# P.V with V as the moving operand in a two-layer decode attention kernel on one core

## Chip, core and metric

The kernel runs on one core of a Trainium2 chip. The metric is the device time of one execution in microseconds; the median of several runs counts.

## What is computed

Eight sequences (B = 8), one new token each, pass twice through an attention block and an MLP block with the same weights and the same K and V caches. D = 512, 32 query heads, 8 KV heads (four query heads share one), 8192 cached positions, head size 128; everything is bf16.

```python
def attention(x):                                  # x: [8, 1, 512]
    q = (x @ wq).reshape(8, 1, 32, 128).transpose(0, 2, 1, 3)
    k, v = repeat(k_cache, 4, axis=1), repeat(v_cache, 4, axis=1)
    p = softmax(einsum("bhqd,bhkd->bhqk", q, k) * 128 ** -0.5)
    return einsum("bhqk,bhkd->bhqd", p, v).transpose(0, 2, 1, 3).reshape(8, 1, 4096) @ wo
def mlp(x):                                        # w1: [512, 1792], w2: [1792, 512]
    return silu(x @ w1) @ w2
for _ in range(2):
    x = x + attention(layernorm(x))
    x = x + mlp(layernorm(x))
```

## The kernel before

The engines are called PE (TensorE), DVE (VectorE), ACT (ScalarE), POOL (GpSimd) and SP (SyncE, which issues the loads of K and V).

**Tasks and steps.** A task is one layer, one sequence and one KV head: 8192 positions, that is 64 chunks of 128. There are 2 x 8 x 8 = 128 tasks. A step handles 8 chunks, so a task has 8 steps (`GPT = 8`, `GRP = 8`). The loop at L616 runs over all steps in one fixed order, and every engine gets its instructions in that order.

**Loads.** K and V come in pieces of 512 KB (16 chunks, two steps) into 27 slots of one arena. A plan made beforehand fixes the order and the slot of each; SP issues a load as soon as the slot's last readers are done. In layer 0, K of the last 18 pieces of a sequence (of 32) stays in its slots, already transposed, and layer 1 uses it again. V is loaded in both layers. Per sequence `make_tasks` orders the tasks so: five tasks of layer 0 whose K is kept, three tasks of layer 1 of the sequence before, three tasks of layer 0 of the next sequence, and then five tasks of layer 1 with the kept K. Those last ones need no transposes, but for half of the first of them.

**A step `p`** gives out, in this order: the transposes of step `p + 3` (`emit_t`, L387: eight chunks of K against the identity into PSUM, from where DVE or ACT copies them back over K in the arena, L393 and L395); the scores of step `p` (`emit_s`, L418: each chunk of transposed K is the stationary operand and 32 query columns move, 4 of which count); P.V of step `p - 12` (`emit_pv`, L468: each chunk of V, 128 positions by 128, is the stationary operand, and four probability columns move); one part of the softmax of the task that has just got its scores; one stage of the chain, if one is open.

**Softmax.** In four steps after a task's last scores: maximum over the chunks on DVE (L427) and over partitions on POOL (L429); subtraction of the maximum on DVE from PSUM into the SBUF tile `SCs` (L436), then the exponential on ACT into `P` (L443); the sum on DVE and POOL; the reciprocal on DVE (L456). `P` has positions on its partitions and (chunk, head) on its columns.

**End of a task.** One step after a task's last P.V, `emit_norm` multiplies the output `OTp` in PSUM (128 head dimensions by 4 heads) by the reciprocal and writes it to `at1` or `at2` (L482).

**The chain.** When the last layer-0 task of a sequence is done, eleven stages are put up: output projection, layer norm, MLP, layer norm and the next query (`chain_of`, with `project` at L536 and `ln_stages`, whose last instruction is L524). One stage is given out a step, among the attention steps, and its matmuls move one column. The second layer of that sequence needs its result.

At the start X is loaded into `Xr` and turned by four small matmuls (L597); at the end the last blocks run for all eight sequences at once, L651 turns the result, and L658 copies it to `Xr` for the store.

Of the kernel before, what the change touches and what calls it, by code (L numbers as in the profile page):

```python
# [7 lines left out]
SM_SCALE = DH ** -0.5  # L8
# [4 lines left out]
GRP = 8  # L13
GPT = 8
# [5 lines left out]
LP = 12  # L20
# [7 lines left out]
BF16 = mybir.dt.bfloat16  # L28
FP32 = mybir.dt.float32
INT32 = mybir.dt.int32  # L30
ACT = mybir.ActivationFunctionType
# [157 lines left out]
def _build(ctx, nc, A_x, A_k_cache, A_v_cache, A_wq, A_wo, B_w1, B_w2, out):  # L189
    B, _sq, D = A_x.shape  # L190
# [3 lines left out]
    REP = HQ // HKV  # L194
    KT = D // 128
    FT = F // 128
    NCH = S // 128
# [10 lines left out]
    NG = len(tasks) * GPT  # L208

    pe = nc.tensor  # L210
    dve = nc.vector
    act = nc.scalar
    pool = nc.gpsimd
    sp = nc.sync
# [3 lines left out]
    def sb(shape, dt, name):  # L218
        _cnt[0] += 1
        return ctx.enter_context(nc.sbuf_tensor(f"{name}_{_cnt[0]}", shape, dt))  # L220

    def ps_bank(name, dt=FP32):
        _cnt[0] += 1
        n = 512 if dt == FP32 else 1024
        return ctx.enter_context(nc.psum_tensor(f"{name}_{_cnt[0]}", [128, n], dt))
# [3 lines left out]
    def chunk(slot, c):  # L229
        o = slot * SLOT + c * 128  # L230
        return ARENA[:, o:o + 128]

    def half(slot, h):
        o = slot * SLOT + h * GRP * 128
        return ARENA[:, o:o + GRP * 128]
# [3 lines left out]
    w1_sb = sb([128, KT, F], BF16, "w1")  # L239
    w2_sb = sb([128, FT, D], BF16, "w2")  # L240
    ident = sb([128, 128], BF16, "ident")
    Xr = sb([128, D], BF16, "X")
    XT = [sb([128, KT, B], BF16, f"XT{n}") for n in range(3)]
    QPAD = SW - REP
    QT1 = sb([128, B * HQ + QPAD], BF16, "QT1")
# [10 lines left out]
    xnT = sb([128, KT, B], BF16, "xnT")  # L256
    eh = sb([128, FT * B], FP32, "eh")
    hsT = sb([128, FT * B], BF16, "hsT")
    SCs = sb([128, NCH * REP], FP32, "SCs")
    Ps = [sb([128, NCH * REP], BF16, "P") for _ in range(NP)]  # L260
    mxp = [sb([128, REP], FP32, "mxp") for _ in range(NST)]
    mxa = [sb([128, REP], FP32, "mxa") for _ in range(NST)]
# [4 lines left out]
    SCp = [ps_bank("SCp") for _ in range(NSCP)]  # L267
    OTp = [ps_bank("OTp") for _ in range(2)]
    TPp = [ps_bank("TPp", BF16) for _ in range(NTP)]
    MISC = ps_bank("MISC")  # L270

    syn = Sync(nc, ctx)
    slsem = [DmaCounter(syn.new_sem(f"sl{i}")) for i in range(NSLOT)]
    wsem = {n: DmaCounter(syn.new_sem(f"w_{n}")) for n in ("wq", "wo", "w1", "w2", "x")}
    osem = syn.new_sem("osem")
# [3 lines left out]
    def res(name):  # L279
        if name not in R:  # L280
            R[name] = Res(name)
        return R[name]

    def r_half(slot, h):
        return res(f"slot{slot}_{h}")

    def op(eng, inst_fn, reads=(), writes=()):
        reads = [res(n) if isinstance(n, str) else n for n in reads]
        writes = [res(n) if isinstance(n, str) else n for n in writes]
        syn.acquire(eng, reads, writes)  # L290
        inst = inst_fn()
        tok = syn.mark(inst, eng)
        syn.release(tok, reads, writes)
        return tok

    def dma(eng, out_ap, in_ap, counter, reads=(), writes=()):
        reads = [res(n) if isinstance(n, str) else n for n in reads]
        writes = [res(n) if isinstance(n, str) else n for n in writes]
        syn.acquire(eng, reads, writes)
        tok = counter.next_tok()  # L300
        eng.dma_start(out_ap, in_ap).then_inc(counter.sem, 16)  # L301
        syn.release(tok, reads, writes)
        return tok

    def mm_group(steps, reads=(), writes=()):
        def run():
            inst = None
            for f in steps:
                inst = f()
            return inst  # L310
        return op(pe, run, reads, writes)

    x_in = A_x.rearrange("b s d -> (b s) d")
    out_v = out.rearrange("b s d -> (b s) d")
# [11 lines left out]
    with nc.Block() as block:  # L326

        @block.sync
        def _(sync_eng):
            dma(sp, Xr[0:B, :], x_in, wsem["x"], writes=["X"])  # L330

            op(pool, lambda: pool.memset(ident[:, :], 1.0), writes=["ident"])
            op(
# [4 lines left out]
                ),  # L338
                reads=["ident"], writes=["ident"],
            )  # L340
            op(pool, lambda: pool.memset(QT1[:, B * HQ:], 0.0), writes=["QT1"])
            for n in range(2):
                op(pool, lambda n=n: pool.memset(QT2[n][:, HQ:], 0.0), writes=[f"QT2_{n}"])
# [3 lines left out]
            def issue_until(pos):  # L347
                while queue and queue[0].after <= pos:
                    issue(queue.pop(0))
# [25 lines left out]
            def where(i):  # L375
                _l, b, g = tasks[i // GPT]
                return b, g, (i % GPT) // GPG, i % GPG
# [19 lines left out]
            def emit_t_until(i):  # L397
                while tnext[0] <= min(i, NG - 1):
                    if has_t(tnext[0]):
                        emit_t(tnext[0])  # L400
                    tnext[0] += 1
# [30 lines left out]
            def softmax_exp(ti):  # L432
                bank, st, pb = ti % NSCP, ti % NST, ti % NP
                op(
                    dve,
                    lambda: dve.tensor_tensor(  # L436
                        SCs[:, :].rearrange("p (c h) -> p c h", h=REP),
                        SCp[bank][:, 0:NCH * REP].rearrange("p (c h) -> p c h", h=REP),
                        mxa[st][:, :].unsqueeze(1).to_broadcast([128, NCH, REP]), ALU.subtract,
                    ),  # L440
                    reads=[f"SC{bank}", f"mxa{st}"], writes=["SCs"],
                )
                op(act, lambda: act.activation(Ps[pb][:, :], SCs[:, :], ACT.Exp, scale=SM_SCALE),  # L443
                   reads=["SCs"], writes=[f"P{pb}"])

            def softmax_sum(ti):
                st, pb = ti % NST, ti % NP
# [10 lines left out]
            def emit_pv(i):  # L458
                ti = i // GPT
                b, g, k, h = where(i)  # L460
                slot = v_slot[(b, g, k)]
                ob, pb = ti % 2, ti % NP
                otp = OTp[ob][:, 0:REP]
                steps = []
                for c in range(GRP):
                    cc = (i % GPT) * GRP + c
                    steps.append(
                        lambda c=c, cc=cc: pe.matmul(  # L468
                            otp, chunk(slot, h * GRP + c), Ps[pb][:, cc * REP:(cc + 1) * REP],
                            start=(cc == 0), stop=(cc == NCH - 1),  # L470
                        )
                    )
                mm_group(steps, reads=[r_half(slot, h), f"P{pb}"], writes=[f"OT{ob}"])

            def emit_norm(ti):
                layer, b, g = tasks[ti]
                ob, st = ti % 2, ti % NST
                if layer == 0:
                    dst, rd = at1[b % 2][:, g * REP:(g + 1) * REP], f"at1_{b % 2}"
                else:  # L480
                    dst, rd = at2[:, g * REP:(g + 1) * REP, b], "at2"
                op(dve, lambda: dve.tensor_tensor(dst, OTp[ob][:, 0:REP], rcp[st][:, :], ALU.mult),  # L482
                   reads=[f"OT{ob}", f"rcp{st}"], writes=[rd])
# [102 lines left out]
            def chain_of(b):  # L586
# [12 lines left out]
                        start=True, stop=True,  # L599
                    )  # L600
                    for kt in range(KT)
                ],
                reads=["X", "ident"], writes=["MISC"],
            )
            op(dve, lambda: dve.tensor_copy(XT[0][:, :, :], MISC[:, 0:KT * B].rearrange("p (k b) -> p k b", b=B)),
               reads=["MISC"], writes=["XT0"])
# [6 lines left out]
            last0 = {b: max(task_at[(0, b, g)] for g in range(HKV)) for b in range(B)}  # L613
            ntask = len(tasks)

            for p in range(NG + LP + GPT + 1):  # L616
                if p < NG:
                    layer, b, _g = tasks[p // GPT]
                    if layer == 1 and chain and chain_b[0] == b:
                        while chain:  # L620
                            chain.pop(0)()
                emit_t_until(p + LT)
                if p < NG:
                    emit_s(p)
                if 0 <= p - LP < NG:
                    emit_pv(p - LP)
                ti, ph = p // GPT - 1, p % GPT
                if 0 <= ti < ntask and ph < 4:
                    (softmax_max, softmax_exp, softmax_sum, softmax_rcp)[ph](ti)
                if chain:  # L630
                    chain.pop(0)()
                done = p - LP - GPT
                if done >= 0 and done % GPT == 0 and done // GPT < ntask:
                    tj = done // GPT
                    emit_norm(tj)
                    layer, b, _g = tasks[tj]
                    if layer == 0 and tj == last0[b]:
                        assert not chain
                        chain.extend(chain_of(b))
                        chain_b[0] = b  # L640
                issue_until(p)
            assert not queue and not chain

            for f in block_stages(
# [10 lines left out]
                ],  # L655
                reads=["XT0", "ident"], writes=["MISC"],
            )
            op(dve, lambda: dve.tensor_copy(Xr[0:B, :], MISC[0:B, :]), reads=["MISC"], writes=["X"])  # L658
            syn.acquire(sp, reads=[res("X")])
            sp.dma_start(out_v, Xr[0:B, :]).then_inc(osem, 16)  # L660
            sp.wait_ge(osem, 16)


# [26 lines left out]
```

## Time and profile before

| | |
|---|---|
| median of 3 runs (lowest to highest) | 1328.16 us (1327.6 to 1328.17) |
| span of the profiled execution | 1321.8 us |
| median less that span | 6.4 us |
| PE busy | 1009.8 us (76%), 25592 matmuls |
| DVE, ACT, POOL busy | 545.3, 328.8, 117.8 us |
| mean granted TensorE clock | 0.739 |
| HBM read | 473.44 MB |
| transposes L387 | 5888 matmuls, 128 moving columns |
| scores L418 | 8192 matmuls, 32 moving columns |
| P.V L468 | 8192 matmuls, 4 moving columns |
| chain and projections L536 | 3312 matmuls, 1 or 8 moving columns |

The profiled execution's own time is listed as its span; a time of the runs includes what lies around it. Matmuls are pipelined: the duration of one is longer than the distance to the next. The granted clock is a share of the full TensorE clock. "Issue" is time in which an engine waited for nothing that the profile shows.

### The profile page before, as it was taken

Reading aid. Unit: us, or ns where it says so; the run is one execution under the profiler, and the core shown is the slowest. Engines: PE = TensorE matmul, PEld = TensorE weight load, DVE = VectorE, ACT = ScalarE, POOL = GpSimd, SP = SyncE. Lnnn points to the kernel's source line nnn. Section 1 sums busy time; section 2 is a strip of 40 time slices with the busy share of each in tenths; the row PEclk is TensorE's granted clock in tenths of the full one; section 3 lists DMA queues with packets and bytes.
Section 4 is the critical chain, followed back from the end, with each engine's and each line's share of the span. In section 5 each row is a group of like instructions: output and inputs, shape, how many; then the busy total and the mean of one; then the engine's idle time right before and its main releaser. Section 6 shows DMA issues by size and latency. Waiting matters only on the chain.

```text
span 1321.8 us, 57028 instructions
## 1 busy us (share of the span) xinstructions
PE 1009.8 (76%) x25592; PEld 983.4 (74%) x25592; DVE 545.3 (41%) x1462; ACT 328.8 (25%) x414; POOL 117.8 (9%) x301
## 2 busy tenths in 40 slices
PE   3758867878677877778778886788867787788875
PEld 3757767877677877778778786787867787788874
DVE  2424434444343533444344442454434454344432
ACT  1323113312132222322123221331313222132210
POOL 0000010000000110000100001000010011000010
PEclk7878658858688776877678675886868867677765
DMA  8999899969999799997999889997999979999892
GB/s 342 386 399 403 291 371 408 377 230 398 408 407 376 256 407 407 408 344 286 408 408 395 303 344 407 408 383 275 377 408 407 388 243 407 407 406 357 287 408 112
DMA packets 133985, 477.14 MB, mean 361 GB/s; under 512 B 14176, under 2 KB 20080, under 8 KB 133232
## 3 DMA queue, kind: packets, MB, share of 16 engines
q1 hardware_dynamic: 133744, 473.51, 92.2%
q8 instruction: 203, 3.33, 1.0%
q14 instruction: 38, 0.31, 0.1%
HBM read 473.44 MB, written 0.01 MB: 358 GB/s over the span
## 4 chain that ended last, share of the span: by engine, by line
PE 53%; DMA 23%; issue 17%; DVE 5%; SPq 1%; POOL 1%; ACT 0%; POOLq 0%; DVEq 0%; ACTq 0%
PE TPp L387 24%; DMA arena<-in_A_k_cache_dram 18%; PE SCp L418 12%; PE OTp L468 11%; PE MISC L536 7%; DMA arena<-in_A_v_cache_dram 3%; SPq L301 1%; DVE arena L395 1%; DMA wq<-in_A_wq_dram 1%; DVE yr L522 1%; DVE tr L520 1%; DVE tr L519 1%; POOL s1a L507 0%; DVE xnT L524 0%; DVE yr L514 0%
## 5 line engine op out<-in xcount | busy, mean ns | idle before, releaser
L387 PE MATMUL TPp<-ident,arena 128*128 128x128 bf16 x5888 | 564.0, 253 | 109.2 <-DMA arena<-in_A_k_cache_dram 70.8
L387 PEld LDWEIGHTS TPp<-ident,arena 128*128 128x128 bf16 x5888 | 425.2, 113 | 117.4 <-DMA arena<-in_A_k_cache_dram 78.7
L395 DVE COPY arena<-TPp 128x1024 bf16<-128x1024 bf16 x460 | 317.3, 690 | 454.7 <-PE TPp L387 452.2
L393 ACT COPY arena<-TPp 128x1024 bf16<-128x1024 bf16 x276 | 278.6, 1010 | 688.6 <-PE TPp L387 688.6
L418 PE MATMUL SCp<-QT,arena 128*128 128x32 bf16 x8192 | 394.2, 184 | 68.6 <-issue 65.6
L468 PE MATMUL OTp<-P,arena 128*128 128x4 bf16 x8192 | 361.0, 165 | 79.3 <-issue 69.7
L418 PEld LDWEIGHTS SCp<-QT,arena 128*128 128x128 bf16 x8192 | 338.8, 103 | 71.0 <-issue 67.5
L468 PEld LDWEIGHTS OTp<-P,arena 128*128 128x128 bf16 x8192 | 290.7, 100 | 91.8 <-issue 81.0
L443 ACT ACTIVATE P<-SCs 128x256 bf16<-128x256 f32 x128 | 53.4, 417 | 271.4 <-DVE SCs L436 216.6
L429 POOL PARTITION_ALL_REDUCE mxa<-mxp x128 | 47.7, 373 | 727.0 <-DVE mxp L427 722.9
L451 POOL PARTITION_ALL_REDUCE ssa<-ssm x128 | 55.2, 431 | 296.4 <-DVE ssm L448 273.9
L427 DVE TENSOR_REDUCE mxp<-SCp 128x4 f32<-128x256 f32 x128 | 53.3, 417 | 46.5 <-PE SCp L418 46.5
L436 DVE TENSOR_TENSOR SCs<-SCp,mxa 128x256 f32<-128x256 f32 x128 | 53.8, 420 | 39.7 <-POOL mxa L429 39.7
L448 DVE TENSOR_REDUCE ssm<-P 128x4 f32<-128x256 bf16 x128 | 53.2, 416 | 41.2 <-ACT P L443 41.2
L536 PE MATMUL MISC<-xnT,wq 128*128 128x1 bf16 (+1 forms) x1152 | 31.8, 165 | 18.3 <-DVE xnT L524 18.2
L536 PEld LDWEIGHTS MISC<-xnT,wq 128*128 128x128 bf16 x1152 | 31.0, 102 | 19.1 <-DVE xnT L524 13.9
L482 DVE TENSOR_TENSOR at<-OTp,rcp 128x4 bf16<-128x4 f32 x128 | 20.0, 156 | 61.0 <-PE OTp L468 61.0
L536 PE MATMUL MISC<-at,wo 128*128 128x1 bf16 (+1 forms) x1152 | 32.5, 165 | 13.0 <-issue 12.7
L536 PEld LDWEIGHTS MISC<-at,wo 128*128 128x128 bf16 x1152 | 31.4, 101 | 13.7 <-issue 13.3
L456 DVE RECIPROCAL rcp<-ssa 128x4 f32<-128x4 f32 x128 | 22.0, 172 | 22.8 <-POOL ssa L451 22.8
L536 PE MATMUL MISC<-xnT,w 128*128 128x1 bf16 (+1 forms) x504 | 14.6, 165 | 18.4 <-DVE xnT L524 18.4
L536 PEld LDWEIGHTS MISC<-xnT,w 128*128 128x128 bf16 x504 | 13.9, 102 | 19.2 <-DVE xnT L524 17.2
(36 smaller groups left out, 111.2 us busy)
## 6 DMA issues: line engine op xcount, KB each, us to landing
arena<-in_A_v_cache_dram SPq DMA_DIRECT2D x512, 512.0 KB, 10.3
arena<-in_A_k_cache_dram SPq DMA_DIRECT2D x368, 512.0 KB, 12.2
wq<-in_A_wq_dram SPq DMA_DIRECT2D x2, 2048.0 KB, 9.4
wo<-in_A_wo_dram SPq DMA_DIRECT2D x1, 4096.0 KB, 26.0
w<-in_B_w_dram SPq DMA_DIRECT2D x2, 1792.0 KB, 22.6
X<-in_A_x_dram SPq DMA_DIRECT2D x1, 8.0 KB
out_dram<-X SPq DMA_DIRECT2D x1, 8.0 KB
```

The source lines that it names most:

```text
L387: lambda c=c: pe.transpose(tpv[:, c, :], chunk(slot, h * GRP + c), ident[:, :])
L393: op(act, lambda: act.copy(dst, TPp[tb][:, :]), reads=[f"TP{tb}"], writes=[r_half(slot, h)])
L395: op(dve, lambda: dve.tensor_copy(dst, TPp[tb][:, :]), reads=[f"TP{tb}"], writes=[r_half(slot, h)])
L418: lambda c=c, o=o: pe.matmul(SCp[bank][:, o:o + SW], chunk(slot, h * GRP + c), rhs, start=True, stop=True,)
L427: op(dve, lambda: dve.tensor_reduce(mxp[st][:, :], scv, AX.X, ALU.max), reads=[f"SC{bank}"], writes=[f"mxp{st}"])
L429: op(pool, lambda: pool.partition_all_reduce(mxa[st][:, :], mxp[st][:, :], 128, bass.bass_isa.ReduceOp.max), reads=[f"mxp{st}"], writes=[f ...
L436: lambda: dve.tensor_tensor(SCs[:, :].rearrange("p (c h) -> p c h", h=REP), SCp[bank][:, 0:NCH * REP].rearrange("p (c h) -> p c h", h=REP) ...
L443: op(act, lambda: act.activation(Ps[pb][:, :], SCs[:, :], ACT.Exp, scale=SM_SCALE), reads=["SCs"], writes=[f"P{pb}"])
L448: op(dve, lambda: dve.tensor_reduce(ssm[st][:, :], Ps[pb][:, :].rearrange("p (c h) -> p h c", h=REP), AX.X, ALU.add), reads=[f"P{pb}"], wr ...
L451: op(pool, lambda: pool.partition_all_reduce(ssa[st][:, :], ssm[st][:, :], 128, bass.bass_isa.ReduceOp.add), reads=[f"ssm{st}"], writes=[f ...
L468: lambda c=c, cc=cc: pe.matmul(otp, chunk(slot, h * GRP + c), Ps[pb][:, cc * REP:(cc + 1) * REP], start=(cc == 0), stop=(cc == NCH - 1),)
L536: lambda o=o, k=k: pe.matmul(MISC[:, o * n:(o + 1) * n], w_sb[:, k, o * 128:(o + 1) * 128], rhs_of(k), start=(k == 0), stop=(k == kparts - 1),
```

## The change

P.V turns round. Four chunks of probabilities, 16 columns (chunk by head), become the stationary operand, and the matching four chunks of V, 512 columns, move past them. A step has two such matmuls instead of eight, and they add up over the task's 64 chunks in 16 partitions by 512 columns of PSUM. Only the four diagonal blocks of this (chunk c of the rows against chunk c of the columns) are wanted. One step after the task's last P.V, DVE copies the 16 x 512 fp32 result to the SBUF tile `OS`; another step later `emit_fold` runs four fp32 matmuls, each with 128 columns of `OS` as the stationary operand and four columns of an fp32 identity, `pick`, moving. They pick the diagonal blocks, add them, and put the 128 x 4 result into the first columns of the same PSUM bank. The multiplication by the reciprocal follows as before.

Beside this, the subtraction of the maximum writes back into the PSUM bank of the scores instead of to `SCs`, and the exponential reads it there. X at the start and the result at the end share the memory of `OS`. The loop runs one step longer, and the chain opens one step later.

```diff
-    Xr = sb([128, D], BF16, "X")
+    PVC = 4
+    pick = sb([PVC * REP, PVC * REP], FP32, "pick")
+    OS = sb([PVC * REP, PVC * 128], FP32, "OS")
+    Xr = OS[:, :].bitcast(BF16)
...
-    SCs = sb([128, NCH * REP], FP32, "SCs")
...
+            op(pool, lambda: pool.tensor_copy(pick[:, :], ident[0:PVC * REP, 0:PVC * REP]), reads=["ident"], writes=["pick"])
...
                     lambda: dve.tensor_tensor(
-                        SCs[:, :].rearrange("p (c h) -> p c h", h=REP),
+                        SCp[bank][:, 0:NCH * REP].rearrange("p (c h) -> p c h", h=REP),
                         SCp[bank][:, 0:NCH * REP].rearrange("p (c h) -> p c h", h=REP),
                         mxa[st][:, :].unsqueeze(1).to_broadcast([128, NCH, REP]), ALU.subtract,
                     ),
-                    reads=[f"SC{bank}", f"mxa{st}"], writes=["SCs"],
+                    reads=[f"SC{bank}", f"mxa{st}"], writes=[f"SC{bank}"],
                 )
-                op(act, lambda: act.activation(Ps[pb][:, :], SCs[:, :], ACT.Exp, scale=SM_SCALE),
-                   reads=["SCs"], writes=[f"P{pb}"])
+                op(act, lambda: act.activation(Ps[pb][:, :], SCp[bank][:, 0:NCH * REP], ACT.Exp, scale=SM_SCALE),
+                   reads=[f"SC{bank}"], writes=[f"P{pb}"])
...
-                otp = OTp[ob][:, 0:REP]
+                otp = OTp[ob][0:PVC * REP, :]
+                rows = half(slot, h)
                 steps = []
-                for c in range(GRP):
+                for c in range(0, GRP, PVC):
                     cc = (i % GPT) * GRP + c
                     steps.append(
                         lambda c=c, cc=cc: pe.matmul(
-                            otp, chunk(slot, h * GRP + c), Ps[pb][:, cc * REP:(cc + 1) * REP],
-                            start=(cc == 0), stop=(cc == NCH - 1),
+                            otp, Ps[pb][:, cc * REP:(cc + PVC) * REP], rows[:, c * 128:(c + PVC) * 128],
+                            start=(cc == 0), stop=(cc + PVC == NCH),
                         )
                     )
...
             def emit_norm(ti):
+                ob = ti % 2
+                op(dve, lambda: dve.tensor_copy(OS[:, :], OTp[ob][0:PVC * REP, :]), reads=[f"OT{ob}"], writes=["OS"])
+
+            def emit_fold(ti):
                 layer, b, g = tasks[ti]
                 ob, st = ti % 2, ti % NST
+                mm_group(
+                    [
+                        lambda c=c: pe.matmul(
+                            OTp[ob][:, 0:REP], OS[:, c * 128:(c + 1) * 128], pick[:, c * REP:(c + 1) * REP],
+                            start=(c == 0), stop=(c == PVC - 1),
+                        )
+                        for c in range(PVC)
+                    ],
+                    reads=["OS", "pick"], writes=[f"OT{ob}"],
+                )
                 if layer == 0:
...
-            for p in range(NG + LP + GPT + 1):
+            for p in range(NG + LP + GPT + 2):
...
                     emit_norm(tj)
+                done -= 1
+                if done >= 0 and done % GPT == 0 and done // GPT < ntask:
+                    tj = done // GPT
+                    emit_fold(tj)
                     layer, b, _g = tasks[tj]
```

## The prediction

> **What bounds the kernel now.** I read the page first. Part 2 shows a repeating pattern in the 40 slices: the transfers run at about 407 GB/s in most slices and dip about once in five. Part 4 says whose work the end waited for.
>
> ```profile
> PEclk7878658858688776877678675886868867677765
> DMA  8999899969999799997999889997999979999892
> GB/s 342 386 399 403 291 371 408 377 230 398 408 407 376 256 407 407 408 344 286 408 408 395 303 344 407 408 383 275 377 408 407 388 243 407 407 406 357 287 408 112
> PE 53%; DMA 23%; issue 17%; DVE 5%; SPq 1%; POOL 1%; ACT 0%; POOLq 0%; DVEq 0%; ACTq 0%
> ```
>
> 408 GB/s is the highest rate any slice reaches; 473.4 MB at it is 1160 us, against a span of 1321.8. The loss must lie in the dips. I cut the span at the first score matmul of each task. Per sequence there are thirteen tasks in which the transfers run without a break (a "steady" stretch) and three tasks (24 steps) in which the small matmul chain of one sequence is threaded between the steps (a "chain" stretch). Two turns, by stretches (us; busy us and instructions of PE, weight loads, DVE, ACT, POOL; granted clock; DMA share; GB/s):
>
> ```profile
> 616.40:730.60 114.20, 88.23 (x2211) 85.71 (x2209) 46.33 (x108) 31.12 (x39) 10.40 (x26) 0.75 1.02 401
> 730.60:774.00 43.40, 36.77 (x948) 36.16 (x946) 19.92 (x70) 10.34 (x13) 4.02 (x10) 0.71 0.76 283
> 774.00:888.40 114.40, 87.34 (x2213) 85.07 (x2211) 47.41 (x110) 30.05 (x38) 10.40 (x26) 0.76 1.02 402
> 888.40:931.30 42.90, 36.25 (x949) 35.72 (x947) 20.09 (x72) 10.31 (x13) 4.00 (x10) 0.68 0.76 281
> ```
>
> The steady stretch is bound by transfers, with 114.2 - 88.2 = 26 us of PE time to spare. The chain stretch is bound by PE, in order and with its waits; the transfers fall to 283 GB/s because loads wait for slots that PE has not freed. The chain of waits prices a step there, in one stretch at half clock and one at full (start us, length us):
>
> ```profile
> 737.34 2.40 PE MISC L536 x94
> 739.74 1.93 issue
> 741.67 1.06 PE MISC L536 x34
> 742.73 0.88 PE TPp L387 x8
> 743.61 0.21 PE SCp L418 x8
> 743.82 0.19 PE OTp L468 x8
> ...
> 771.13 0.47 PE TPp L387 x8
> 771.60 0.19 PE SCp L418 x8
> 771.79 0.19 PE OTp L468 x8
> ```
>
> Eight transposes move 8 x 128 = 1024 columns: 0.47 us at full clock, 0.88 at half. Eight score matmuls cost 0.19 to 0.21 at either clock, and so do eight of today's P.V (4 columns each): these are paced by instruction, about 25 ns a pair, not by columns. A step is 0.85 or 1.28 us. The 1.93 us "issue" is PE waiting for instructions.
>
> What sets the clock is visible in the transposes alone, by stretches of 3.4 us (PE busy and count; granted clock; DMA share; GB/s):
>
> ```profile
> 749.20:752.60 3.40, 1.29 (x11) 0.50 0.84 320
> 752.60:756.00 3.40, 1.49 (x15) 0.50 0.38 106
> 756.00:759.40 3.40, 2.60 (x23) 0.50 0.67 231
> 759.40:762.80 3.40, 0.43 (x7) 1.00 0.98 369
> 762.80:766.20 3.40, 1.01 (x8) 0.50 0.62 239
> ```
>
> The clock changes on such stretches, one after its cause: 23 transposes are followed by full clock, 7 to 15 by half. Counting the score columns in, the border lies near 3,200 moved columns per stretch. Tasks without transposes run at 0.50.
>
> **P.V (L468 becomes two matmuls a step).** Removed: 8 weight loads of 128 columns and 8 matmuls, 0.19 to 0.21 us a step. Added: 2 loads of 16 columns and 2 matmuls of 512 columns, which is 1024 columns, exactly what the transposes of a step move. So I price it like them: 0.47 at full clock, 0.88 at half. Narrow stationary operands do not change that rate: the last matmuls, L651, put four times 128 columns past 8 stationary columns at 107 ns spacing at half clock, as the transposes have it. A step with transposes becomes 0.47 + 0.19 + 0.47 = 1.13 (was 0.85), at half clock 0.88 + 0.21 + 0.88 = 1.97 (was 1.28); a step without, 0.66.
>
> Instructions fall from 48 to 36 a step. In tasks without transposes PE now takes 256 instructions per 6.2 us and idles some 2.4 us of that on issue; at 20 per 0.66 us the new kernel needs 5.3 us a task plus the fold, so this wait mostly goes, but it lies in a stretch bound by transfers and pays nothing there. In the chain stretch I take the 1.93 us as saved once, since the queue is then no longer drained before the chain arrives (0 to 1.9).
>
> **Clock.** A half-clock step moves 1024 + 256 + 1024 = 2304 columns in 1.97 us, some 4,000 per 3.4 us, over the border; at the transfers' pace of a task per 10.3 us it is 6,100. So steady stretches run at full clock. In the chain stretch one-column matmuls and waits (16.1 us of its 43.4) still drop it: I take 7 of 24 steps at half clock, where about 11 are now.
> [...]
>
> **Fold (four fp32 matmuls a task, plus a copy on DVE).** The copy of 16 x 512 is like L658 (8 x 512, 0.68 us): 128 x 0.68 = 87 us on a DVE that is 41% busy, issued a whole step before PE's fold, so one step of PE work (1.13 or 0.66) covers it; uncovered it would cost up to 0.7 us a task. Behind it in DVE's queue lie the next evacuations, which have three transpose buffers of slack. DVE's multiply now waits for the fold as it waited for P.V. No row shows fp32 on PE. Lower end: L597 (8 x 128 stationary, bf16), 27 ns each, 0.1 us a fold. [...] I take 16 pairs at the transposes' full-clock pitch of 55 ns, 0.9 us, because loads with 128 columns pitch like that when columns set the pace.
>
> **One-answer edits.** Shift in PSUM: DVE reads PSUM in L427 and SBUF in L448 at the same 416 ns, so 0 +- 0.1 us, off the path; the score bank is held 0.5 us longer, its next writer is seven steps away. `pick` copy: once, before the first score. X sharing OS: both uses far apart. One more loop step: the last copy and fold, 0.68 + 0.9 = 1.6 us at the end. The chain starts one step later: it has a step of room.
>
> **The sum**, against the profiled span of 1321.8:
> - Steady (104 steps, 68 with transposes, 13 folds): 68 x 1.13 + 36 x 0.66 + 13 x 0.9 = 76.8 + 23.8 + 11.7 = 112.3, against 114.2 measured. Still just under the transfers; with 1.9 us of slack instead of 26, I add 3 us for waits that no longer overlap (0 to 6). Seven such stretches: +21.
> - Chain: 16.1 stay, less 1.9 fetch, less 0.6 (two waits for DVE's L524, each covered 0.28 longer); 24 x 1.13 = 27.1; 7 x 0.84 = 5.9 for half clock; 3 folds 2.7. Total 49.3 against 43.4: +5.9, eight times: +47.
> - End: +1.6.
> Together 1321.8 + 70 = 1392. The median 1328.16 lies 6.4 above the span: 1398. With a fold of 0.1: no steady loss, chain +3.5, 1357. With 1.8: 124.0 steady (+9.8), chain +8.6, 1468.
>
> **Rivals.**
> [...]
> - *Switching costs a drain.* P.V alone uses 16 stationary columns, twice a step the shape changes. At 24.75 the last transpose starts and L597, of another shape, starts 0.247 later, not 0.107: 0.14 late. For one such per step, steady is 126.9 and chain +9.3: 1493; for two, 1621. Against: L597 also waits on another semaphore.
> [...]
> - *Faster.* The chain stretch becomes cheaper because denser columns hold the full clock through it: 16.1 - 2.5 + 27.1 = 40.7, plus three folds and 0.84 for each half-clock step, falls under 43.4 once these stay under 2.7 us. With a fold of 0.1 and one such step it is 41.8, -1.6 eight times: 1316. For: about 11 steps are at half clock now. Against: the one-column matmuls remain.
> - *Half clock throughout*, if 16 of 128 columns count for little activity: steady 68 x 1.97 + 36 x 1.09 + 13 x 1.5 = 193, chain 65.4: about 2050.
>
> **How the numbers follow.** Forecast 0.54, fold dear 0.18, drain 0.12, half clock 0.05, faster 0.08, no change (within 0.2%, which is about what a measurement of this kernel can tell) 0.03. The range, 1325 to 1540, leaves out faster, half clock and the upper half of the drain: 0.19. The forecast's own range is 1340 to 1470. Slower by over 0.2%: 0.89.
>
> **What would show it.** Right: P.V as 2048 matmuls at 0.44 to 0.47 us a pair, PEclk near 0.9 or more in steady stretches and lower in the chain's, steady stretches still near 400 GB/s, chain stretches near 49 us, fewer issue waits. Wrong: PE with no idle time and under 380 GB/s in steady stretches (fold or drain), gaps at each change between S and P.V (drain), PEclk at 0.5 (half clock), chain stretches under 43 us (faster).

## The result, and the profile after

The changed kernel takes 1500.55 us (median of 4 runs, 1496.91 to 1502.82) against 1327.88 for the kernel before: 1.1293 times as long, 95% interval 1.1272 to 1.1314. Its profiled execution took 1499.54 us with a span of 1497.7, 175.9 more than the span before.

The same rows of the page as before, for the changed kernel:

```profile
PEclk7999899989999899989999899997999999998897
DMA  8998698779978799678997799976998779967790
GB/s 346 380 408 330 228 410 314 273 249 383 409 284 283 285 393 408 243 263 303 401 405 243 249 356 410 347 274 207 377 408 314 280 271 392 408 247 280 263 391 9
PE 92%; DVE 4%; DMA 3%; issue 1%; POOL 0%; SPq 0%; POOLq 0%; ACT 0%; DVEq 0%
```

The clock is up to 0.946 on average, from 0.739. The transfers fall below 300 GB/s in 18 of the 40 slices (before, in 8), and 92% of the chain of waits is PE (before, 53%). The stretches, cut at the same tasks as before (steady, chain, steady, chain):

```profile
510.60:639.70 129.10, 129.10 (x1692) 80.65 (x1690) 56.88 (x122) 29.45 (x38) 10.41 (x26) 1.00 0.92 352
639.70:691.10 51.40, 48.24 (x827) 34.35 (x825) 22.03 (x73) 10.23 (x13) 3.98 (x10) 0.87 0.72 248
691.10:820.20 129.10, 129.10 (x1692) 80.64 (x1690) 55.79 (x119) 30.41 (x39) 10.41 (x26) 1.00 0.92 350
820.20:868.40 48.20, 46.15 (x829) 33.12 (x827) 21.85 (x73) 10.15 (x13) 4.00 (x10) 0.89 0.76 264
```

A steady stretch takes 129.1 us where it took 114.2, with PE busy in every one of them and the transfers at 350 GB/s: there the bound has moved from the transfers to PE. A chain stretch takes 48.2 to 53.6 us (seven of them, mean 50.3) where it took 43.8 on average. Together the seven chain stretches give 45.9 of the 175.9 us and six steady stretches 91.0; the first steady stretch, which holds the first chain too, gives 22.6, and the start and the end 16.5. One step with transposes and one fold, PE's matmuls in order of time (start us, length us; a length runs to the modelled end of the last matmul, so steps are read from start to start):

```profile
602.22 1.05 PE L488 MATMUL OTp<-pick,OS 16*128 16x4 f32 x8
603.20 0.62 PE L390 MATMUL TPp<-ident,arena 128*128 128x128 bf16 x8
603.66 0.35 PE L421 MATMUL SCp<-QT,arena 128*128 128x32 bf16 x8
603.95 0.60 PE L472 MATMUL OTp<-arena,P 128*16 128x512 bf16 x2
604.48 0.62 PE L390 MATMUL TPp<-ident,arena 128*128 128x128 bf16 x8
```

The fold takes 603.20 - 602.22 = 0.98 us and appears as eight fp32 pairs, two for each matmul in the source. The step takes 1.28 us: transposes 0.46, scores 0.29, P.V 0.53. Over a task it is 1.273 on average. The parts that are new against the prices in the prediction are 0.10 us more for the scores, whose matmuls are unchanged, and 0.06 for P.V. The weight loads show where this is (start, length, idle time before):

```profile
609.57 0.45 PEld L390 LDWEIGHTS TPp<-ident,arena 128*128 128x128 bf16 x8 [0.43 <-issue]
609.97 0.31 PEld L421 LDWEIGHTS SCp<-QT,arena 128*128 128x128 bf16 x8
610.31 0.10 PEld L472 LDWEIGHTS OTp<-arena,P 128*16 128x16 bf16 x2
610.84 0.23 PEld L390 LDWEIGHTS TPp<-ident,arena 128*128 128x128 bf16 x4 [0.43 <-issue]
```

The single records say that the first P.V matmul starts 0.105 us after the last score matmul, where score matmuls follow each other at 0.025; the second follows at 0.220; and the next transpose starts 0.311 us after that. So before P.V 0.08 us are lost (0.105 against 0.025), after it 0.09 (0.311 against 0.220). The loads of the other shape are not drawn ahead of the matmul in flight: the load at 610.84 starts with its own matmul, 0.31 us after the last P.V matmul, where inside the group of transposes a load starts 0.002 us after the matmul in front.

### The profile page after: what moved, and what is told of

Read it like the earlier page. It is cut to its first block, busy times and chain, and to the rows that moved or that the text cites. A ratio compares the mean times of both kernels' runs of the same rounds, so it can differ in the third digit from the quotient of the medians.

```text
span 1497.7 us, 46822 instructions
## 1 busy us (share of the span) xinstructions
PE 1433.7 (96%) x20472; PEld 934.1 (62%) x20472; DVE 636.5 (42%) x1590; ACT 322.7 (22%) x414; POOL 117.9 (8%) x302
## 4 chain that ended last, share of the span: by engine, by line
PE 92%; DVE 4%; DMA 3%; issue 1%; POOL 0%; SPq 0%; POOLq 0%; ACT 0%; DVEq 0%
PE OTp L472 36%; PE TPp L390 27%; PE SCp L421 15%; PE OTp L488 8%; PE MISC L554 6%; DMA arena<-in_A_k_cache_dram 2%; DMA wq<-in_A_wq_dram 1%; DVE arena L398 1%; DVE tr L538 1%; DVE yr L540 1%; DVE tr L537 1%; DVE xnT L542 0%; DVE yr L534 0%; DVE yr L532 0%; SPq L303 0%
## 5 line engine op out<-in xcount | busy, mean ns | idle before, releaser
L472 PE MATMUL OTp<-arena,P 128*16 128x512 bf16 x2048 | 631.4, 391 | 0.9
L390 PEld LDWEIGHTS TPp<-ident,arena 128*128 128x128 bf16 x5888 | 349.2, 101 | 298.9 <-issue 275.2
L390 PE MATMUL TPp<-ident,arena 128*128 128x128 bf16 x5888 | 477.8, 227 | 24.4 <-DMA arena<-in_A_k_cache_dram 14.3
L421 PEld LDWEIGHTS SCp<-QT,arena 128*128 128x128 bf16 x8192 | 306.8, 97 | 117.1 <-PE SCp L421 89.1
L488 PEld LDWEIGHTS OTp<-pick,OS 16*128 16x128 f32 x1024 | 124.8, 188 | 56.6 <-issue 51.8
L488 PE MATMUL OTp<-pick,OS 16*128 16x4 f32 x1024 | 135.9, 252 | 0.8 <-DVE OS L481 0.8
L472 PEld LDWEIGHTS OTp<-arena,P 128*16 128x16 bf16 x2048 | 99.3, 87 | 38.7 <-PE OTp L472 3.4
L446 ACT ACTIVATE P<-SCp 128x256 bf16<-128x256 f32 x128 | 49.4, 386 | 331.4 <-DVE SCp L439 331.4
L481 DVE COPY OS<-OTp 16x512 f32<-16x512 f32 x128 | 86.2, 674 | 35.8 <-PE OTp L472 35.8
L439 DVE TENSOR_TENSOR SCp<-SCp,mxa 128x256 f32<-128x256 f32 x128 | 54.9, 429 | 38.3 <-POOL mxa L432 38.2
L554 PEld LDWEIGHTS MISC<-at,wo 128*128 128x128 bf16 x1152 | 29.7, 97 | 3.8 <-issue 3.5
```

The source lines that it names most:

```text
L390: lambda c=c: pe.transpose(tpv[:, c, :], chunk(slot, h * GRP + c), ident[:, :])
L421: lambda c=c, o=o: pe.matmul(SCp[bank][:, o:o + SW], chunk(slot, h * GRP + c), rhs, start=True, stop=True,)
L439: lambda: dve.tensor_tensor(SCp[bank][:, 0:NCH * REP].rearrange("p (c h) -> p c h", h=REP), SCp[bank][:, 0:NCH * REP].rearrange("p (c h) - ...
L472: lambda c=c, cc=cc: pe.matmul(otp, Ps[pb][:, cc * REP:(cc + PVC) * REP], rows[:, c * 128:(c + PVC) * 128], start=(cc == 0), stop=(cc + PV ...
L481: op(dve, lambda: dve.tensor_copy(OS[:, :], OTp[ob][0:PVC * REP, :]), reads=[f"OT{ob}"], writes=["OS"])
L488: lambda c=c: pe.matmul(OTp[ob][:, 0:REP], OS[:, c * 128:(c + 1) * 128], pick[:, c * REP:(c + 1) * REP], start=(c == 0), stop=(c == PVC - 1),)
```

## Experiments

The theory: each change of the number of stationary columns, two a step, costs one of these gaps, 0.08 and 0.09 us. (That PE runs empty in them was the author's estimate: the ends of matmuls are modelled, so the trace shows the gaps, and the loads held back, but not an empty PE.) The rivals: the gaps belong to the long 512-column matmul, or to any load of fewer than 128 columns, or to each group of P.V matmuls.

**128 stationary columns.** The stationary operand is widened to 128 columns of `P`; the rows above 16 are not read.

```diff
-    Ps = [sb([128, NCH * REP], BF16, "P") for _ in range(NP)]
+    PW = 128
+    Ps = [sb([128, NCH * REP + PW - PVC * REP], BF16, "P") for _ in range(NP)]
...
-                otp = OTp[ob][0:PVC * REP, :]
+                otp = OTp[ob][0:PW, :]
...
-                            otp, Ps[pb][:, cc * REP:(cc + PVC) * REP], rows[:, c * 128:(c + PVC) * 128],
+                            otp, Ps[pb][:, cc * REP:cc * REP + PW], rows[:, c * 128:(c + PVC) * 128],
```

> P.V has 128 stationary columns instead of 16 (28 more chunks' probabilities, zeros beyond the task's end); only the first 16 output rows are read. Theory A (changing the number of stationary columns twice a step empties PE, 0.08 to 0.10 us each way): the gaps before and after P.V go, a step falls from 1.273 to about 1.12 us, the steady stretch from 129.0 to about 114 to 117 us (13 folds of 0.98 stay), the chain stretch by 3.5, the time to about 1375 to 1395. Theory B (the gaps belong to the long 512-column matmul, whatever its stationary operand): step and time unchanged, about 1500.

Measured: 1357.7 us, 1.0224 [1.0183, 1.0264] times the kernel before. The weight loads again, and one steady and one chain stretch:

```profile
600.18 0.36 PEld L424 LDWEIGHTS SCp<-QT,arena 128*128 128x128 bf16 x8
600.47 0.12 PEld L475 LDWEIGHTS OTp<-arena,P 128*128 128x128 bf16 x2
600.71 0.65 PEld L393 LDWEIGHTS TPp<-ident,arena 128*128 128x128 bf16 x8
```

```profile
630.50:742.60 112.10, 111.99 (x1691) 84.05 (x1689) 55.58 (x120) 30.40 (x39) 10.41 (x26) 1.00 1.02 399
742.60:791.20 48.60, 45.61 (x828) 36.55 (x826) 21.82 (x73) 10.15 (x13) 4.00 (x10) 0.82 0.76 272
```

The same 512-column matmuls now follow the scores at 0.025 us and are followed at 0.215; the next load starts at 600.71, 0.21 us ahead of its matmul. A task with transposes takes 9.72 us instead of 11.17, and the steady stretch is with the transfers again (399 GB/s). The rival of the long matmul falls. The time came out 17 us lower than the range: the steady stretch is some 2 us and a step 0.04 us shorter than I took. The chain stretches fell by only 1.5 us (to 48.8), not by 3.5.

**96 and 64 columns** (`PW = 96`, `PW = 64`, nothing else).

> As the run with 128 columns, but with 96. [...] Theory A2 (any count but 128 loads in another way, and that load is not drawn ahead): gaps as with 16, about 1500, or more by the longer load.

> P.V with 64 stationary columns. [...]

Measured: 1375.8 us with 96 (1.0362 [1.0344, 1.038]) and 1518.0 with 64 (1.1422 [1.1397, 1.1446]). PE in one step, first 96, then 64:

```profile
640.76 0.35 PE L424 MATMUL SCp<-QT,arena 128*128 128x32 bf16 x8
640.97 0.61 PE L475 MATMUL OTp<-arena,P 128*96 128x512 bf16 x2
641.41 0.61 PE L393 MATMUL TPp<-ident,arena 128*128 128x128 bf16 x8
```

```profile
601.03 0.35 PE L424 MATMUL SCp<-QT,arena 128*128 128x32 bf16 x8
601.32 0.62 PE L475 MATMUL OTp<-arena,P 128*64 128x512 bf16 x2
601.87 0.34 PE L393 MATMUL TPp<-ident,arena 128*128 128x128 bf16 x3
```

With 96, scores to P.V is 0.21 us and P.V to transposes 0.44; with 64 they are 0.29 and 0.55, much as with 16 (0.29 and 0.53). So it is not any load under 128 columns, and the border lies between 64 and 96. (96 columns cost 0.02 us a step more than 128. The trace has it between the two matmuls of a P.V group, 0.232 us apart instead of 0.215; why, was not tried.) The gaps are 0.17 us together for a pair of changes with 16 columns; why 16 and 64 columns have them and 96 and 128 do not, no run shows.

**Half as many changes of shape.** P.V of two steps is given out in every second step, with 16 columns.

```diff
-                if 0 <= p - LP < NG:
-                    emit_pv(p - LP)
+                if 0 <= p - LP < NG and (p - LP) % 2 == 1:
+                    emit_pv(p - LP - 1)
+                    emit_pv(p - LP)
```

> The changed kernel with 16 stationary columns, P.V of two steps given out together in every second step: half as many changes of shape, the same matmuls. If each change empties PE (0.105 to 0.025 us before P.V and 0.307 to 0.216 after it, 0.17 together), a step is 0.085 shorter on average: a task 11.17 to 10.5, without transposes 7.59 to 6.9, the steady stretch 129.1 to 120 to 121, the time about 1415. If the gap belongs to each group of P.V matmuls, all stays at 1500.

```profile
622.39 1.25 PE L472 MATMUL OTp<-arena,P 128*16 128x512 bf16 x4
```

Measured: 1567.0 us (1.1812 [1.1757, 1.1867]), slower than the changed kernel, against every expectation. The second group's first matmul started 0.437 us after the last of the first group: the group waits on PE's own semaphore for the last writer of its PSUM bank, which now is the group just in front. The line above shows the four matmuls taking 1.25 us. With one step between them, in the changed kernel, that wait shows 6 times in the whole span, 3.4 us together. Tasks without transposes lose most by it, 8.61 us against 7.59, since there the score groups of two steps also stand next to each other. The next run took it away by giving out all four matmuls as one group, `emit_pv(p - LP - 1, p - LP)`:

> As the run before it (P.V of two steps together, 16 stationary columns), but the four matmuls are one group with one wait in front: there, the second pair of a group waited for the first to end (0.437 us between their starts instead of 0.216), since it writes the same PSUM bank and PE waits for its own semaphore. Half as many changes of shape: a pair of steps 2 x 1.273 - 0.17 = 2.38 us, a task 10.5, without transposes 6.9, the steady stretch 120 to 121, the time about 1415. If the gap doesn't belong to the change of shape: 1500.

```profile
585.65 0.62 PE L390 MATMUL TPp<-ident,arena 128*128 128x128 bf16 x8
586.11 0.35 PE L421 MATMUL SCp<-QT,arena 128*128 128x32 bf16 x8
586.31 0.61 PE L390 MATMUL TPp<-ident,arena 128*128 128x128 bf16 x8
586.76 0.35 PE L421 MATMUL SCp<-QT,arena 128*128 128x32 bf16 x8
587.04 1.03 PE L473 MATMUL OTp<-arena,P 128*16 128x512 bf16 x4
588.00 0.62 PE L390 MATMUL TPp<-ident,arena 128*128 128x128 bf16 x8
```

Two steps take 588.00 - 585.65 = 2.35 us instead of 2.55, and a task 10.38 instead of 11.17: one pair of changes saved is 0.20 us. Scores followed by transposes cost 0.20, scores followed by P.V 0.28. The time is 1453.8 (1.0947 [1.0912, 1.0982]), above the 1415 expected, because tasks without transposes take 7.71 us and not 6.9; there two score groups now follow each other directly in one bank. The trace shows the same wait: the second group's weight loads stand idle for 0.16 us until the first group's scores are done, and its first matmul starts 0.236 us after the last of the first group instead of 0.025, four times a task.

**The fold in bf16.** `OS` is bf16 and `ident` takes the place of `pick`.

> The fold alone is changed: OS is bf16 (the partial sums are rounded to it) and the bf16 identity takes the place of pick. If the fold's 0.98 us are its eight fp32 load-and-multiply pairs of 0.112 us, four bf16 pairs of 0.027 us plus the two switches leave 0.3 us: steady stretch 129.0 to 120, chain stretch 2 less, time about 1420. If the switches into and out of the fold are most of it, it stays over 0.6 us and the time over 1450. P.V's step of 1.273 us is the same either way.

Measured: 1406.4 us (1.0609 [1.0575, 1.0644]). A task falls from 11.17 to 10.37 us, the steady stretch from 129.1 to 118.7.

```profile
597.55 0.25 PE L488 MATMUL OTp<-ident,OS 16*128 16x4 bf16 x4
597.73 0.62 PE L390 MATMUL TPp<-ident,arena 128*128 128x128 bf16 x8
```

The bf16 fold leaves 0.18 us, less than the 0.3 expected, so fp32 was 0.8 of the 0.98. Some 0.07 of the 0.18 is a change of shape too: the fold has 128 stationary columns but only 16 rows, and its last matmul is followed after 0.092 us, where a fold of 128 rows (the version without any change of shape, below) is followed after 0.025.

**The score shift alone**, in the kernel before.

```diff
-                        SCs[:, :].rearrange("p (c h) -> p c h", h=REP),
+                        SCp[bank][:, 0:NCH * REP].rearrange("p (c h) -> p c h", h=REP),
...
-                op(act, lambda: act.activation(Ps[pb][:, :], SCs[:, :], ACT.Exp, scale=SM_SCALE),
+                op(act, lambda: act.activation(Ps[pb][:, :], SCp[bank][:, 0:NCH * REP], ACT.Exp, scale=SM_SCALE),
```

> The kernel before with one part of the change alone: the maximum is subtracted inside PSUM and the exponential reads PSUM. All theories: on no path, 1328 within 3 us.

Measured: 1328.9 us, 1.0007 [0.9991, 1.0022]. It plays no part. The subtraction takes 429 ns instead of 420, the exponential 385 instead of 417.

**No change of shape at all.** 128 columns in P.V, and a fold that keeps the shape too:

```diff
-    OS = sb([PVC * REP, PVC * 128], FP32, "OS")
+    OS = sb([128, PVC * 128], BF16, "OS")
...
-                op(dve, lambda: dve.tensor_copy(OS[:, :], OTp[ob][0:PVC * REP, :]), reads=[f"OT{ob}"], writes=["OS"])
+                op(dve, lambda: dve.tensor_copy(OS[:, :], OTp[ob][:, :]), reads=[f"OT{ob}"], writes=["OS"])
...
-                            OTp[ob][:, 0:REP], OS[:, c * 128:(c + 1) * 128], pick[:, c * REP:(c + 1) * REP],
+                            OTp[ob][:, 0:REP], OS[:, c * 128:(c + 1) * 128], ident[:, c * REP:(c + 1) * REP],
```

> 128 stationary columns in P.V and a fold that changes no shape either: DVE copies all 128 rows to a bf16 OS, and the four folding matmuls take 128 rows by 128 columns against four columns of the bf16 identity, whose rows beyond 16 are zero there. If what is left over the kernel before is the fold: 0.99 + 0.09 us fall to 4 x 0.026 = 0.1, a task with transposes from 9.72 to 8.75, the chain stretch by 3 (48.8 to 45.8), the steady stretch stays with the transfers (112 to 113), about 1330 to 1336. If the chain stretch doesn't get shorter, the fold wasn't on its path, and the time stays near 1355.

Measured: 1312.7 us, 0.9881 [0.9858, 0.9904] times the kernel before, so faster than it, and 17 us under the time expected. The idea of the change does pay once its two costs are gone.

```profile
615.00:726.60 111.60, 102.16 (x1613) 71.69 (x1640) 55.76 (x120) 30.40 (x39) 10.40 (x26) 1.00 1.02 404
726.60:768.90 42.30, 37.99 (x805) 31.07 (x814) 21.78 (x73) 10.15 (x13) 4.00 (x10) 0.92 0.84 307
```

The steady stretches take 111.2 us on average (six), bound by transfers with 9 us of PE time to spare, the chain stretches 44.8 (seven, 42.3 to 49.2) at up to 307 GB/s; each is about 1 us less than expected.

**Denser columns in the chain.** The chain's matmuls move 32 columns, 31 of which are overwritten or unused, in the kernel before and in the last version. The core of the edit, in `project` (the operands are widened to match):

```diff
+                w = CW if n == 1 else n        # CW = 32
...
-                                MISC[:, o * n:(o + 1) * n], w_sb[:, k, o * 128:(o + 1) * 128], rhs_of(k),
+                                MISC[:, o * n:o * n + w], w_sb[:, k, o * 128:(o + 1) * 128], rhs_of(k),
```

> The kernel before, whose chain matmuls move 32 columns instead of one (31 of each result are overwritten or unused). Theory (the clock of a 3.4 us window follows from the columns moved in the one before, with a border near 3,200): 128 chain matmuls move 4,096 columns in their 3.4 us, the clock holds through more of the chain stretch, PEclk there rises from 0.70 to 0.8 or more, the stretch falls from 43.8 to 38 to 41, the time to 1290 to 1312. Rival (the clock falls because PE waits, or one-column matmuls are counted like others): unchanged within 0.5%.

> Both: no change of shape in P.V and fold, and 32 columns in the chain. By the theory the chain stretch is 16.1 + 24 x 1.08 + 0.3 less 2 = 40 at full clock, some half-clock steps on top: 40 to 43, the time 1300 to 1320. If the clock doesn't follow the columns: as the same kernel with one column in the chain.

```profile
612.80:727.80 115.00, 87.86 (x2211) 84.95 (x2209) 46.39 (x108) 31.21 (x39) 10.40 (x26) 0.78 1.02 403
727.80:769.20 41.40, 34.50 (x947) 34.06 (x946) 19.72 (x70) 10.44 (x13) 4.02 (x10) 0.79 0.79 285
```

```profile
605.20:716.80 111.60, 101.83 (x1611) 71.66 (x1638) 55.76 (x120) 30.41 (x39) 10.41 (x26) 1.00 1.02 405
716.80:758.10 41.30, 36.76 (x807) 30.10 (x816) 21.77 (x73) 10.15 (x13) 4.00 (x10) 0.96 0.84 306
```

Measured: 1317.4 us (0.9912 [0.989, 0.9935]) in the kernel before, 1296.9 (0.9762 [0.9743, 0.9781]) together with the version without changes of shape; the latter is the fastest of all, 3 us under the range expected of it. The pitch of the chain's matmuls stays at 0.026 us, so the 31 columns cost nothing, and the clock rises from 0.69 to 0.82 in the kernel before and from 0.88 to 0.95 in the version without changes of shape (means over seven chain stretches). So the clock follows the moved columns and not the number of matmuls, which is the same.

The traces say where the border lies. They list the granted clock in windows of 3.41 us. With each matmul counted in the window in which it starts, a border of 3,150 moved columns in one window tells the clock of the next in 375 of 386 windows of the kernel before and in 431 of 438 of the changed one. The best border on PE's busy time fails in 105 and 34 windows, so it is not that PE waits.

The first gain is smaller than expected: 1317.4 against 1290 to 1312. The mean clock rose as forecast, but the chain stretch fell only from 43.8 to 41.8 us, not to 38 to 41. PE still waits for DVE before two of the chain's projections, 2.2 to 2.5 us each in one chain stretch of the trace, and these waits grew by 0.7 us a chain stretch. And of the 2.0 us gained there the steady stretches give 1.2 back (115.2 against 113.9). The rates fit this: a chain stretch now moves 12.0 MB instead of 12.4, and the rest is left for a stretch that is bound by transfers. This account is read from the traces; no run tried it by itself.

## Why the prediction went wrong

**Direction, clock and bound: right.** PEclk is 1.00 in the steady stretches. The border of some 3,200 moved columns also pointed the right way for 32 columns in the chain. Sixteen stationary columns count like 128: tasks without transposes, where P.V moves four of five columns, run at 1.00, and the half-clock rival is gone.

**The step that failed** is "So I price it like them: 0.47 at full clock", P.V by the transposes, with nothing for the change between them. It put a step at 1.13 us and left a cost of switching, its rival "drain", at 0.12. The price of the columns was right and even high (0.43 us for two matmuls with 128 stationary columns, 0.47 taken). What was missing is the change of shape, 0.17 us: a step is 1.273. By the terms of the sum, a steady stretch is 68 x 1.273 + 36 x 0.826 + 13 x 0.98 = 86.6 + 29.7 + 12.7 = 129.0, against 129.1 measured and 112.3 summed. Of the 16.7 us between them, steps with transposes give 9.7, steps without 6.0, and the folds 1.0. The prediction had found a sign, L597 starting 0.14 us late, and its rival with one such delay a step came to 1493. That this is near the 1500 measured is in part luck: the 0.14 was read at half clock and at a change of rows (L597 has 8 of 128), while the delay here is 0.17 for two changes of columns. The sign was set aside because L597 also waited on another semaphore; that L651's columns kept their pitch was taken as proof for a narrow operand, but L651 came after a wait of PE and could show no change of shape.

**What the missing term did.** With 1.9 us of slack left in a steady stretch, every further cost went through to the end: the steady stretches, where I had +3 each, gave about +15 each (the first, with its chain, 22.6). It is shown by removal: with 128 columns, and the fold left as it is, the steady stretch is 112.1 to 114.0.

**The fold: right in size.** 0.98 us against 0.9, made of 8 pairs of 0.112 rather than 16 of 0.055. No run shows the 16 pairs behind the 0.9, or a fold of 1.8 us: the trace has two pairs for each fp32 matmul.

**The chain stretch: right in sum.** 49.3 forecast, 50.3 on average. The 0.14 us a step that were missing were made up in part by fewer steps at half clock, about 4.8 of 24 where I took 7. The 1.8 us a chain stretch that PE had waited for instructions are gone, as the sum had it (in the 1.93 us from 739.74 on in the kernel before, a 16 KB packet of the instruction queue is under way from 739.36 to 740.46).

**The 6.4 us around the span** were too much: in the later profiles a run is some 1.8 above its own span (1499.54 and 1497.7 here), so before's profiled execution was simply shorter than the median run.

**The faster rival** was an option of the idea, not of this code. Its condition, folds and half-clock steps together under 2.7 us, is met in the version with the same shape everywhere by three chain stretches of seven (42.3 to 42.5 us, under 43.4), but not on average (44.8). Its gain came from another place: the steady stretches fell from 113.9 to 111.2 us. A chain stretch there moves 13.0 MB instead of 12.4, and so the steady stretch has less left to move. This last reading rests on the rates alone and was not tried by itself.

## What to carry to other kernels

Before narrowing the stationary operand, count how often PE changes between a wide and a narrow one: here each pair of changes between 128 and 16 cost 0.17 to 0.20 us, more than a third of the 0.43 us of P.V between them, and padding to the wide shape with columns nobody reads cost no time (0.215 us from one P.V matmul to the next, 0.220 with 16). A stretch that is bound by transfers with PE time to spare (26 of 114.2 us here) hides a good deal, but once a sum lands within 2% of the other bound, any term left at zero decides the case. A weak sign in the trace that speaks for a rival deserves its price in the sum when the rival's place occurs a thousand times.

## What the runs showed of the hardware

- With 16 stationary columns between groups of 128, at full clock, the first matmul of 16 starts 0.105 us after the last of 128 (0.025 where both have 128), and the first of 128 starts 0.311 us after the last of 16, its weight load with it (0.215 where both have 128, the load 0.21 us ahead). With 64 columns the way from scores to P.V and from P.V to transposes is as long, 0.29 and 0.55 us against 0.29 and 0.53; with 96 it is 0.21 and 0.44, with 128 some 0.20 and 0.43. From 16 rows back to 128, with 128 columns in both, costs 0.067 us (0.092 against 0.025).
- An fp32 matmul with 128 stationary and four moving columns shows as two load-and-multiply pairs, 0.112 us apart at full clock; the same in bf16 shows as one, and four of them take 0.10 to 0.11 us where no shape changes.
- The clock changes in windows of 3.41 us with the columns moved in the window before, past 16 stationary columns as past 128: a border of 3,150 columns tells the clock in 375 of 386 windows of the kernel before and in 431 of 438 of the changed one.
- When PE waits on its own semaphore for the matmul just before, the overlap of the two is lost: 0.437 us from start to start instead of 0.220 for 512 moving columns, 0.236 instead of 0.025 for 32.
